# A new engine order, searched over sampled transfer delays, and Silu's table loaded by the first activation

## The chip, the cores and the metric

The kernel runs on one core of a Trainium2 chip. The metric is the device time of one execution in microseconds (us), as the median of several runs. A run is called fast or slow by how it stands to the fastest run of the same kernel, and only fast runs are compared.

## The reference

One sequence of 2048 rows with 640 columns in bfloat16 goes through two blocks, each with a residual:

```python
def _A_ref(q, k, v, shift_k, ssm_k, ssm_D):
    k_shift = ...                       # causal 4-tap filter of k along the sequence, per column
    kv = k_shift * v
    kv_f = rfft2(pad(kv));  kf_f = rfft2(pad(ssm_k))
    y = irfft2(kv_f * kf_f)[:S]         # long convolution along the sequence, per column
    return q * (y + kv * ssm_D)

def _B_ref(x, w_gate, w_up, w_down):    # 640 -> 1728 -> 640
    return (silu(x @ w_gate) * (x @ w_up)) @ w_down

h  = A_q + _A_ref(layernorm(A_q), A_k, A_v, A_shift_k, A_ssm_k, A_ssm_D)
h2 = h + _B_ref(layernorm(h), B_w_gate, B_w_up, B_w_down)
```

## The kernel before

The sequence is cut into four blocks of 512 rows. For each block the kernel forms the key-value product (`kv`), takes it through the long convolution as matmuls with transform tables, multiplies by the normalised query, normalises again and runs the feed-forward network (FFN). Between two matmul stages of the convolution the intermediate is written back to on-chip memory in another layout by small DMA transfers. I call these **reshuffles**; SyncE issues them. The convolution's filter goes through the same kind of transfer (the **filter shuffles**). A step of ACT or DVE that copies a matmul's result out of its accumulation memory is called an **evacuation**. A_k, A_v and A_q are the loads of a block's inputs.

Nothing is issued while the Python code walks through the computation. Each step is recorded with its engine, a cost, and what it reads and writes. Then a list scheduler places the steps by rank. A table of 1616 ranks and a string that fixes which of ScalarE (ACT) or VectorE (DVE) does a step were found by a search and are written into the source:

```python
_ORDER = """
156 113 119 17 19 112 121 158 111 118 482 590 193 ...     # [cut: 1616 ranks]
"""
_WHO = ("....d..ad.da.dd......................................."  # [cut]
)
...
for r, i in enumerate(_ORDER.split()):
    P.ops[int(i)].prio = r
for o, w in zip(P.ops, _WHO):
    o.force = {"a": "act", "d": "dve"}.get(w)
P.schedule(0.8)
```

The costs (in us) and the transfer's assumed times stand where a step is recorded. Nearly all steps go through such helpers, which is why the profile shows L681 for most matmuls, L672 for most transfers and L891 for most vector work:

```python
def dma(subs, kb, reads, writes, prio, eng="sp", ..., kind="load", w=None):
    return P.op({eng: (0.9 if eng == "pool" else 0.62 if kind == "shuffle" else 0.5) * len(subs)}, fns, reads, writes, prio,
                dma=((w or kb / 390.0), ..., 0.8 if kind != "load" else 1.5), name=name)

# reciprocal square root of a LayerNorm: GpSimd (POOL), between two small DVE steps va and nm
P.op({"pool": 1.05}, lambda g: g.tensor_tensor(out=y, in0=va, in1=..., op=ALU.pow), ..., name=f"nr{l}{j}")
```

The third part that matters is the key-value product of blocks 2 and 3. Three of its four taps are added by DMA, not by an engine: GpSimd issues a transfer of 320 KB that adds while it writes. The DVE step `kvv`, which multiplies by v, needs the last of these:

```python
def acc(src, cells):
    P.op({"pool": 1.0}, [lambda g: g.dma_start(v4(t0), src(), accum_op=ALU.add)],
         [(t0, 0)] + cells, [(t0, 0)], prio, dma=(2.1, 2.1, 0.8), name=f"kvd{j}{c}")
...
acc(lambda: v4(t1), [(t1, 0)])
mul(t1, 2)
... # tap 3, on DVE
acc(lambda: kw(0), [(kt, c)])
acc(lambda: v4(t1), [(t1, 0)])                     # the third: kvv waits for it
vec(dve2(W4), tt(hv, hv, lambda: v4(t0), ALU.mult), [(t0, 0), (vt, c)] + ..., name=f"kvv{j}{c}")
```

The FFN's gate goes through ACT's Silu (`si`), and DVE multiplies by the other half (`gm`).

Of the kernel before, what the change touches and what calls it, by code (L numbers as in the profile page):

```python
# [16 lines left out]
156 113 119 17 19 112 121 158 111 118 482 590 193 1380 1412 1519 464 211 432 1142 466 1146 485 1418 1408 1322 1321 53 22 1108 1134 24 28 1143 1350 87  # L17
1509 25 205 1 1377 1243 955 1430 1346 73 1347 642 153 21 30 27 29 134 798 43 63 71 167 110 115 106 9 536 57 654 956 794 1250 217 75 82 93 100 84 952
65 12 1247 376 26 3 56 97 379 378 129 102 162 760 1111 91 20 2 1121 23 15 1162 1318 1300 1354 1410 1426 130 61 31 269 406 373 37 128 96 381 450 410
588 596 492 59 6 416 501 1118 69 1330 1434 1308 528 516 518 1338 802 801 1130 163 98 86 127 546 1233 1416 542 165 1448 538 499 664 704 1031 151 67 90  # L20
941 942 225 1251 685 784 1045 550 933 1086 1096 714 228 540 548 1175 1406 1319 264 274 1444 527 169 1456 621 370 1481 1013 1381 183 728 719 669 1424
135 147 139 231 452 455 531 903 346 690 226 229 1087 985 792 999 680 1011 694 431 437 208 81 245 817 243 791 192 544 772 300 319 294 256 186 724 783
184 182 827 835 1266 1258 585 979 665 1254 1256 1264 1260 695 1009 1007 709 675 392 511 238 467 261 1114 408 420 557 32 689 699 1028 407 367 239 230
202 670 920 917 201 421 213 204 198 191 45 4 1104 790 257 244 189 598 399 423 987 415 576 137 356 782 787 786 679 1001 418 255 251 227 977 529 459
1228 1348 1109 1344 461 1116 159 232 108 469 1362 1316 1312 224 446 442 178 99 149 206 168 514 200 1043 700 387 397 55 223 524 458 426 209 267 468 428
160 141 417 517 197 526 263 520 143 171 199 190 1113 414 443 219 582 1168 157 120 1349 1172 203 1443 1357 1441 447 483 710 411 0 448 796 64 60 477 377
409 1465 1438 1351 506 389 393 487 246 1314 412 368 1141 58 1457 1352 595 809 480 500 1409 1244 1242 581 398 438 177 390 535 534 222 216 215 1274 270
1227 131 150 686 495 1119 764 556 375 207 558 241 240 247 254 1371 1364 1363 1171 564 566 577 575 1372 170 266 36 486 35 70 85 1570 154 34 1212 386
1569 276 286 1433 161 1403 117 385 775 502 145 403 507 498 572 441 1374 493 565 681 424 242 1058 470 1565 522 103 503 975 401 770 530 221 1442 1436
181 391 454 369 769 766 301 944 295 938 419 220 439 395 701 939 947 394 396 388 465 237 142 473 471 497 1563 1150 253 296 641 474 935 891 860 605 608  # L30
607 579 402 814 196 549 551 249 472 974 1440 1496 435 1040 1413 800 479 478 78 52 1089 1091 768 1353 218 433 543 1117 508 851 1432 1313 1492 1178 236
1139 1446 767 578 574 803 496 822 781 726 1063 1067 1065 973 644 328 315 1262 306 553 563 950 316 951 88 427 614 1471 1369 1345 1342 777 532 1360 1472
1466 321 314 547 613 1240 820 823 661 552 1166 1458 647 829 1439 337 855 863 1216 862 155 1485 525 212 696 1238 1464 1462 1428 1239 1358 1236 1234 505
567 374 521 523 1488 284 265 706 281 1411 1205 656 449 586 776 404 1615 774 1514 587 811 806 876 360 1588 1177 333 364 1167 425 258 456 1420 773 490
325 457 1473 195 146 233 148 948 599 476 512 324 275 268 1069 18 271 857 1487 845 11 491 949 444 771 210 895 214 1419 250 326 1523 1597 1486 1606 1453
405 365 555 1066 721 413 33 640 252 899 72 39 248 422 906 136 133 1309 1068 1084 475 1226 172 653 639 1094 1310 570 632 865 617 627 904 825 912 889 68
94 913 1106 1107 1102 1098 429 1608 305 991 989 901 897 1248 635 957 62 5 1187 101 515 881 1421 911 545 74 797 638 460 430 1375 235 589 481 969 623
930 929 1399 436 650 1246 651 1224 821 628 1217 778 965 853 309 988 440 462 83 1218 1221 655 868 636 38 92 76 591 282 914 910 907 887 1245 1378 66
1241 637 434 400 1463 1020 1235 1366 1367 1138 1468 937 1290 878 338 1037 932 509 180 351 877 793 893 659 886 981 41 819 504 843 779 445 1014 976 185
510 176 166 114 174 1497 831 756 953 609 666 867 1215 842 291 780 610 606 997 494 1291 1270 995 996 1220 1230 1140 924 1607 513 350 573 1269 1271 1272  # L40
859 14 849 164 844 1469 280 1027 871 892 347 962 1057 1041 940 705 902 890 928 1030 453 1095 1049 8 272 259 262 716 896 888 1407 353 7 1315 841 1252
915 982 619 1547 1535 1555 1263 1268 691 795 711 1257 1024 676 980 990 992 123 1103 671 925 1016 1082 126 1105 1093 788 1017 1376 1083 1081 1078 1578
1567 879 451 1577 1341 47 1382 840 1267 1015 916 1451 984 1079 173 89 175 122 1259 1261 1101 657 116 40 152 620 80 921 909 884 882 559 484 946 344
1025 519 959 625 900 894 1035 931 354 1021 1005 1018 1019 852 846 1059 1023 838 1002 986 1566 936 934 463 1155 905 604 815 290 1524 304 1072 1388 1214
1196 1255 1265 1551 1559 684 785 1527 285 1543 1158 1126 674 918 187 1539 1449 1197 805 561 124 971 1292 1219 50 873 874 77 125 537 799 1475 48 16 260
13 1003 1511 1460 1201 1522 1452 1286 1225 789 10 51 109 132 1000 569 629 1513 1454 1185 667 662 46 49 1115 1311 1004 138 1298 194 140 1253 1574 1323
1289 1326 1122 188 660 1611 54 601 1154 1211 594 600 663 107 1199 1223 278 1573 541 1561 1553 1558 1470 382 539 279 371 273 380 105 95 597 42 584 603
593 299 1537 612 615 104 1202 384 383 289 922 1229 1538 1557 1188 1181 1123 44 1609 1542 1222 1437 1429 1132 1033 1549 571 813 1459 372 1144 1541 1525
919 978 1306 1294 1355 1288 179 144 1404 1332 1074 1127 725 1398 1053 804 908 807 288 1401 1032 826 1076 1180 1505 1343 618 488 1427 630 1384 751 1278
355 489 993 983 1602 1279 1560 1572 1540 737 1529 1546 1110 366 234 1526 1213 1055 927 926 1237 1530 1550 1533 1302 1071 1075 1276 812 1287 1285 1385  # L50
568 1589 1151 1159 1135 624 970 960 964 1545 1249 866 643 583 1435 533 562 818 668 1593 1534 1562 580 1170 1390 1280 1386 1414 1008 677 1478 1373 1198
968 1128 998 1392 277 850 1394 1284 283 808 592 1333 1006 687 1450 611 954 898 1152 358 864 312 626 634 707 298 560 602 287 311 1186 1507 682 810 1010
297 1584 1595 854 292 828 1422 1336 832 967 293 302 883 830 816 652 313 885 317 836 303 824 834 308 858 1317 943 861 692 330 733 673 1012 1528 307
1585 318 327 966 331 738 1402 1077 340 322 323 958 972 1174 622 357 648 335 1482 1581 848 363 361 339 1328 1592 1383 1397 342 672 1050 678 872 336
1594 875 348 341 1461 945 1232 1048 1026 683 658 717 722 1598 1590 688 1415 1603 693 362 334 646 343 856 697 359 1320 1455 713 1554 332 1029 712 1173
1423 698 1044 702 703 1042 727 649 645 1387 1277 1393 1467 1164 1120 1080 1064 708 349 345 1334 755 746 1389 554 1340 352 1275 1056 1604 718 1613 1612
723 1092 961 1304 1052 748 765 1061 740 750 1165 1039 1169 1296 739 1359 735 1281 837 310 1176 1293 1301 1283 1273 1400 747 1370 1361 1060 741 754 994
1073 1160 1099 1508 749 1070 1054 833 633 631 1512 1521 1136 1516 1517 869 729 1062 1022 870 1034 1124 1580 1137 1447 1161 1391 1324 1046 1556 1153
1145 880 1356 1231 1112 1038 1299 1297 1335 734 715 1088 1305 1327 1325 1295 1395 1303 1036 1575 1379 736 1183 1192 1282 1051 732 731 1100 1148 1097
1480 1133 1484 1208 1194 1206 1491 1489 1090 1368 1190 753 1189 1193 1156 1531 1396 744 743 1179 752 329 1586 1582 1571 1600 1591 730 923 759 1047  # L60
1498 1479 1515 1125 1510 1085 1207 1329 1331 1579 1307 1157 1337 1149 1417 1425 742 720 1500 763 745 847 1599 1203 1339 757 758 1131 1445 839 320 616
1200 963 1474 1147 1204 1209 1191 1477 1520 1476 1163 1483 1182 1499 1493 1502 1494 1501 1490 1184 1195 1518 1504 1506 1129 1495 1503 79 1431 1405
1210 1564 762 761 1605 1601 1583 1610 1536 1532 1548 1552 1568 1614 1596 1587 1576 1365 1544
"""
_WHO = (
# [456 lines left out]
def bass_sequential_preLN__ssm_conv_h3__swiglu_ffn__prompt_kernel(  # L522
# [28 lines left out]
    P = Prog()  # L551
# [812 lines left out]
```

## Time and profile before

| | before |
|---|---|
| median, us (3 runs) | 313.04 (311.83 to 314.07) |
| span of the profiled run, us | 310.9 |
| TensorE (PE) busy, us | 284.1 (91%) |
| DVE busy, us | 243.3 (78%) |
| ACT busy, us | 194.2 (62%) |
| GpSimd (POOL) busy, us | 29.5 |
| mean granted PE clock (1 is full speed) | 0.989 |

PE is the busiest engine, but not the bound all the time. Up to about 60 us DVE is full and PE waits for it; from 210 us on PE alone is full; in between the engines hand work to each other, and a stretch of the timeline has to be read for the wait that ends last in it. The prediction below shows the stretches, the waits of the worst one and the chain that explains them. One pair of lines it does not show becomes important later. It is from the waits over the whole span (who waited for whom: us in total, times, longest us):

```profile
PE ps L681 <- DMA sb<-sb: 8.8, 9, 2.9
DVE sb L891 <- DMA sb<-sb: 4.1, 3, 2.1
```

PE loses 8.8 us to transfers within the on-chip memory, and DVE loses 4.1 us.

### The profile page before, as it was taken

The page shows a single profiled execution, that of the slowest core. Times are in us where ns is not written, and L with a number is a line of the kernel's source. Part 1 is how long each engine was busy: PE and PEld are TensorE (multiplying, and loading weights), DVE is VectorE, ACT ScalarE, POOL GpSimd, SP SyncE. Part 2 cuts the span into 40 slices and gives each one's busy share as a digit, 9 for nine tenths or more (in the row PEclk, how much of TensorE's full clock was granted, in tenths as well). Part 3 has the DMA queues.
Part 4 walks back from the last instruction along what each step waited for, and adds up shares of the span by engine and source line. Part 5 has one row for each costly group of instructions (what it writes and reads, how often), then busy time and mean ns, then how long its engine had stood idle before and what let it go on. Part 6 is the DMA issues. An engine that isn't in the chain of part 4 may idle for free.

```text
span 310.9 us, 5160 instructions
## 1 busy us (share of the span) xinstructions
PE 284.1 (91%) x1804; PEld 152.7 (49%) x1804; DVE 243.3 (78%) x493; ACT 194.2 (62%) x450; POOL 29.5 (9%) x34
## 2 busy tenths in 40 slices
PE   3799887989989989999499999989999999999995
PEld 1466554434534456653234465534444576444563
DVE  5899999988799969998759999996599672313421
ACT  3389999998877626986668985695983220332100
POOL 2101102031101204200101020200010010000000
PEclk9999999899999999999979999999999999999999
DMA  7999996748907795558500261674201105000002
GB/s 209 362 373 273 364 358 216 235 113 203 234 3 211 147 289 115 129 159 228 142 1 2 84 126 44 233 132 146 86 0 42 44 20 128 23 0 0 2 14 71
DMA packets 42473, 43.24 MB, mean 139 GB/s; under 512 B 14848, under 2 KB 37056, under 8 KB 42320
## 3 DMA queue, kind: packets, MB, share of 16 engines
q1 hardware_dynamic: 38974, 38.30, 40.2%
q0 software_dynamic: 3328, 3.97, 8.0%
q10 hardware_dynamic: 146, 0.66, 0.6%
q8 instruction: 14, 0.23, 0.3%
q14 instruction: 11, 0.09, 0.1%
HBM read 20.63 MB, written 2.62 MB: 75 GB/s over the span
## 4 chain that ended last, share of the span: by engine, by line
PE 55%; DVE 18%; DMA 15%; ACT 5%; SPq 3%; issue 2%; POOL 0%; DVEq 0%; ACTq 0%; POOLq 0%
PE ps L681 54%; DVE sb L891 15%; DMA sb<-sb 13%; SPq L672 3%; ACT sb L664 3%; DMA sb<-in_A_ssm_k_dram 2%; ACT sb L1027 1%; DVE stt L981 1%; DVE sb L665 1%; PE ps L798 1%; PE ps L1199 1%; DVE sb L1153 1%; POOL stt L997 0%; ACT L1223 0%; ACT sb L1223 0%
## 5 line engine op out<-in xcount | busy, mean ns | idle before, releaser
L681 PE MATMUL ps<-sb 128*128 128x320 bf16 (+2 forms) x1204 | 224.7, 340 | 8.6 <-POOL stt L970 2.8
L891 DVE TENSOR_TENSOR sb<-sb 128x1280 bf16<-128x1280 bf16 (+3 forms) x270 | 166.0, 672 | 8.5 <-DMA sb<-sb 4.1
L681 PEld LDWEIGHTS ps<-sb 128*128 128x128 bf16 (+2 forms) x1204 | 115.0, 99 | 101.8 <-issue 8.4
L664 ACT ACTIVATE sb<-ps 128x320 bf16<-128x320 f32 (+2 forms) x246 | 100.4, 489 | 38.9 <-PE ps L681 32.9
L681 PE MATMUL ps<-sb,tab 128*64 128x320 bf16 (+2 forms) x512 | 66.4, 309 | 12.2 <-DMA sb<-sb 7.7
L891 DVE TENSOR_TENSOR sb<-ps,sb 128x320 bf16<-128x320 f32 (+2 forms) x70 | 38.6, 572 | 43.3 <-PE ps L681 31.1
L1223 ACT ACTIVATE sb<-ps 128x512 bf16<-128x512 f32 (+1 forms) x56 | 33.5, 602 | 37.2 <-PE ps L681 37.1
L681 PEld LDWEIGHTS ps<-sb,tab 128*64 128x64 f16 (+2 forms) x512 | 32.0, 102 | 46.7 <-issue 15.2
L1007 ACT ACTIVATE sb<-sb,stt 128x320 bf16<-128x320 bf16 (+1 forms) x40 | 28.2, 739 | 11.2 <-DVE stt L999 11.1
L997 POOL TENSOR_TENSOR stt<-stt 128x2 f32<-128x2 f32 (+1 forms) x12 | 13.5, 1124 | 120.7 <-DVE stt L996 66.7
L665 DVE CAST sb<-ps 128x320 bf16<-128x320 f32 x41 | 19.0, 482 | 5.7 <-PE ps L681 5.5
L1067 POOL DMA_DIRECT2D sb<-sb x12 | 12.2, 1016 | 78.1 <-DVE sb L891 57.4
L667 ACT ACTIVATE sb<-ps 128x320 bf16<-128x320 f32 x42 | 16.3, 459 | 4.4 <-PE ps L681 4.1
L981 DVE BATCH_NORM_STATS2 stt<-sb 128x6 f32<-128x320 bf16 x32 | 14.2, 476 | 0.0
L1027 ACT ACTIVATE sb<-sb,stt 128x640 bf16<-128x640 bf16 x16 | 13.4, 835 | 0.5 <-DVE stt L1023 0.5
L1020 ACT ACTIVATE sb<-sb 128x640 bf16<-128x640 bf16 x16 | 11.9, 746 | 1.4 <-DMA sb<-in_A_q_dram 1.4
L798 PE MATMUL ps<-sb 128*128 128x128 bf16 (+1 forms) x48 | 4.0, 231 | 2.2 <-DMA sb<-in_A_ssm_k_dram 2.1
L798 PEld LDWEIGHTS ps<-sb 128*128 128x128 bf16 (+1 forms) x48 | 3.2, 120 | 3.7 <-DMA sb<-in_A_ssm_k_dram 2.7
L1199 PE MATMUL ps<-sb 128*128 128x128 bf16 x40 | 4.1, 242 | 0.6 <-DVE sb L1006 0.6
L809 POOL TENSOR_TENSOR sb<-sb 1x320 bf16<-1x320 bf16 x2 | 2.2, 1108 | 24.1 <-ACT sb L664 17.5
L1199 PEld LDWEIGHTS ps<-sb 128*128 128x128 bf16 x40 | 2.8, 106 | 2.5 <-DVE sb L1006 0.8
L668 DVE TENSOR_SCALAR sb<-ps 128x320 bf16<-128x320 f32 x6 | 2.9, 489 | 0.9 <-PE ps L681 0.9
(23 smaller groups left out, 29.3 us busy)
## 6 DMA issues: line engine op xcount, KB each, us to landing
sb<-sb SPq DMA_DIRECT2D x72, 160.0 KB, 2.2
sb<-sb POOLq DMA_DIRECT2D x12, 320.0 KB, 4.3
out_dram<-sb SPq DMA_DIRECT2D x16, 160.0 KB, 2.0
sb<-in_A_k_dram SPq DMA_DIRECT2D x8, 280.0 KB, 4.2
sb<-in_B_w_down_dram SPq DMA_DIRECT2D x13, 160.0 KB, 7.2
sb<-cst_den SPq DMA_DIRECT2D x8, 256.0 KB, 7.8
sb<-in_A_q_dram SPq DMA_DIRECT2D x6, 320.0 KB, 4.5
sb<-in_A_v_dram SPq DMA_DIRECT2D x6, 320.0 KB, 5.5
```

Of the source, the lines that this page charges most:

```text
L664: fns = {"act": lambda a: a.activation(out=dst(), in_=src(), func=ACTF.Copy), "dve": lambda v: v.tensor_copy(out=dst(), in_=src())}
L665: "dve": lambda v: v.tensor_copy(out=dst(), in_=src())}
L667: fns = {"act": lambda a: a.activation(out=dst(), in_=src(), func=ACTF.Copy, scale=scale), "dve": lambda v: v.tensor_scalar(out=dst(), in0 ...
L681: return lambda t: t.matmul(o(), l(), r(), start=st, stop=sp)
L891: return lambda v: v.tensor_tensor(out=o(), in0=a(), in1=b_(), op=op)
L981: vec(dve1(CW, False), lambda v: v.bn_stats(st6(l, j, b, c), V(xt, b * D + c * CW, CW)), [(xt, (b, c))], [(ST, ("s", l, j, b, c))], prio, ...
L997: P.op({"pool": 1.05}, lambda g: g.tensor_tensor(out=y, in0=va, in1=stt[:, 420:420 + hi - lo], op=ALU.pow), c1 + [(ST, "half")], c3, prio, ...
L1007: "act": lambda a: a.activation(out=dst(), in_=src(), func=ACTF.Identity, scale=rs(l, j, b), bias=tmv(l, j, 3)[:, b:b + 1])},
L1020: P.op({"act": act_c(D) + 0.22}, lambda a, b=b, jt=jt: a.activation(out=V(jt, 0, D), in_=V(xt, b * D, D), func=ACTF.Copy, accum_out=tmv(l, ...
L1027: P.op({"act": act_c(D) + 0.3}, lambda a, b=b, jt=jt: a.activation(out=V(jt, 0, D), in_=V(xt, b * D, D), func=ACTF.Square, bias=tmv(l, j, ...
L1067: P.op({"pool": 1.0}, [lambda g: g.dma_start(v4(t0), src(), accum_op=ALU.add)], [(t0, 0)] + cells, [(t0, 0)], prio, dma=(2.1, 2.1, 0.8), n ...
L1223: P.op({"act": act_c(n)}, lambda a: a.activation(out=dst(), in_=src(), func=ACTF.Silu), rd, wr, -1000, name=f"si{nm}", after=after)
```

## The change

The intent: the search that makes the order no longer minimises the span for one nominal set of transfer times. It minimises the mean span over samples of them, so that an order that is fast only if each transfer takes its nominal time is marked down. Three costs that the scheduler assumes are raised, and a tiny Silu is put ahead of everything, so that ACT loads Silu's table while nothing waits for it.

```diff
 _ORDER = """
-156 113 119 17 19 112 121 158 111 118 482 590 193 ...    [cut: all 1616 ranks]
+59 1571 1566 12 3 1574 93 71 61 1575 1570 73 57 ...      [cut: all 1617 ranks]
 _WHO = (
-    "....d..ad.da.dd....."   [cut]
+    ".....a.a..ad.aa....."   [cut: seven steps change from DVE to ACT, net]
@@ def dma
-  ... 0.8 if kind != "load" else 1.5), name=name)
+  ... 0.8 if kind != "load" else 2.0 if name[0] in "xv" or name[:3] == "kin" else 1.5), name=name)
@@ def ln_rstd
-            P.op({"pool": 1.05}, lambda g: g.tensor_tensor(... op=ALU.pow), ...
+            P.op({"pool": 1.2}, lambda g: g.tensor_tensor(... op=ALU.pow), ...
@@ def acc
-                P.op({"pool": 1.0}, [lambda g: g.dma_start(v4(t0), src(), accum_op=ALU.add)],
+                P.op({"pool": 1.35}, [lambda g: g.dma_start(v4(t0), src(), accum_op=ALU.add)],
@@ def load_weights
+            P.op({"act": 0.3}, lambda a: a.activation(out=V(WD, 13 * D, 8, 64, 128), in_=V(WD, 13 * D, 8, 64, 128), func=ACTF.Silu),
+                 [(WD, (13, "z"))], [(WD, (13, "z"))], -3000, name="sil0")
```

## The prediction

> **What bounds the kernel now.** The list of busy times on the profile's page comes first: TensorE (PE) is busy 284.1 of 310.9 us, so at most 26.8 us of the span has an idle PE, and no new order can take more than that plus what PE loses while it counts as busy. The second view cuts the span into stretches and shows when it is idle; its columns are the stretch, its length, then the busy time and (instructions) of PE, weight loads, DVE, ACT, POOL, then clock, DMA share and GB/s.
>
> ```profile
> 0.00:10.00 10.00, 3.80 (x20) 1.88 (x20) 5.72 (x12) 3.30 (x5) 2.35 (x9) 1.00 0.81 236
> 10.00:60.00 50.00, 45.04 (x315) 27.39 (x316) 49.37 (x110) 42.42 (x105) 5.37 (x5) 0.97 1.00 320
> 60.00:130.00 70.00, 65.26 (x428) 33.75 (x428) 62.85 (x127) 52.73 (x122) 12.37 (x11) 1.00 0.63 155
> ...
> 140.00:160.00 20.00, 14.57 (x76) 5.71 (x74) 14.02 (x25) 11.88 (x30) 0.84 (x1) 0.91 0.52 144
> 160.00:190.00 30.00, 29.96 (x189) 15.61 (x189) 29.81 (x57) 26.80 (x65) 3.40 (x3) 1.00 0.24 55
> 190.00:210.00 20.00, 17.84 (x139) 10.12 (x136) 19.51 (x46) 14.31 (x35) 1.92 (x2) 1.00 0.60 160
> 210.00:300.00 90.00, 89.92 (x527) 46.95 (x528) 49.10 (x102) 33.55 (x69) 2.37 (x3) 1.00 0.14 42
> 300.00:311.00 11.00, 7.70 (x57) 5.31 (x55) 2.95 (x6) 0.00 (x0) 0.00 (x0) 1.00 0.17 60
> ```
>
> Length less PE busy gives the idle ledger: 6.2 us at the start, 5.0 in 10-60, 4.7 in 60-130, 5.4 in the twenty microseconds 140-160, 2.2 in 190-210, 3.3 at the end, and nothing in the rest. Start and end (first loads; last evacuation and store) are hardly open to an order. In 10-60 DVE is busy 49.4 of 50 us and ACT 42.4, so there PE waits for vector work. From 210 to 300 PE alone is the bound. The stretch to read closely is 140-160. The waits of that stretch (who waited for whom: total us, times, longest):
>
> ```profile
> PE ps L681 <- DMA sb<-sb: 5.4, 2, 2.9
> ...
> DVE sb L891 <- DMA sb<-in_A_v_dram: 2.7, 1, 2.7
> ACT sb L1020 <- DMA sb<-in_A_q_dram: 1.4, 1, 1.4
> ```
>
> All its PE idleness is two waits for on-chip reshuffles (the transposes of the convolution's intermediate between its stages). The chain of waits says why they were late:
>
> ```profile
> 144.13 0.55 SPq L672
> ...
> 144.78 5.27 DMA sb<-sb
> ...
> 150.13 0.56 SPq L672
> 150.74 0.60 SPq L672
> 151.38 0.61 SPq L672
> ...
> 152.03 4.12 DMA sb<-sb
> ```
>
> A reshuffle has a median of 2.2 us from issue to landing in the table of issues; these took 5.27 and 4.12. The timeline shows SyncE issuing A_q loads at 139.71 and A_v loads at 143.06, just ahead of them in the same queue. There is a second loss that PE's busy share hides: the clock column reads 0.91 there. 46 matmuls of 512 columns took 12.0 us in 140-160 (261 ns each), against 48 in 10.5 us in 270-280 (219 ns): 46 x 0.042 = 1.9 us. So the stretch loses 5.4 + 1.9 = 7.3 us.
>
> The table load of Silu is one row, taken from the source view of that line:
>
> ```profile
> L1223 ACT ACT_TABLE_LOAD  x1: 1283/1283/1283, 61.6 to 61.6; - x1
> ```
>
> It stands in the chain that ended last, at 61.58, in a stretch (60-70) where ACT was busy 9.97 of 10 us; soon after it PE waits for ACT 0.67 and 0.37 us (66.12 and 66.94).
>
> **What the Trainium skill says.** "ScalarE: Activation LUTs", section "What ACT_TABLE_LOAD costs", gives about 1283 ns for the load plus about 1380 ns of drain for every switch of set. The trace agrees on the load (1283 ns, twice) and shows no drain: the previous ACT item ended at 61.57, the load began at 61.58, and the first Silu followed at 62.88. I use 1.28 us. "DMA: Bandwidth & Descriptors", in the latency part on where the ~2 us go, puts a small transfer at about 2 us fixed; the 2.2 us median agrees. The same page, "Queues, rings and completion order", says that on each DMA engine descriptors are consumed in ring order; the 5.27 us of a reshuffle issued behind four large loads agrees. "TensorE: Matmul & The Clock Gate", Part 1, says that an idle window of about 3.4 us halves the PE clock until a busy window follows; the 0.91 behind gaps of 2.9 and 2.5 us fits, though neither gap is a whole window.
>
> **The change part by part.** The work is the same: 500 PE steps in both orders, 493 DVE steps become 486 and 418 ACT steps 426 (eight evacuations change hands, one Silu on eight columns is new). The three altered cost constants only feed the scheduler. What moves is order, and I read it by counting the matmuls that stand between two points on PE, at 0.219 us per 512 columns and 320/512 of that (0.137) for 320.
>
> 1. *The loads ahead of block 2's last reshuffles.* The A_v buffer comes free when the last stage-1 matmul of block 2 has read it. Before, from there to the second pair of inverse transforms stand two groups of five 512-column matmuls and one pair: 2.5 us. In the new order stand nine 320-column, twenty 512-column and ten 320-column matmuls: 1.2 + 4.4 + 1.4 = 7.0 us. Besides, the four 80 KB shuffles of the next filter, which stood mixed among the loads on SyncE at 0.6 us an issue, now follow the reshuffles: 2.4 us of issue out of the way. So the loads should be down before the reshuffles are issued. The reshuffle itself still has only 4.4 us of PE work to hide behind (4.9 before), and its own path is an evacuation (0.5), issues (0.6 each, two) and 2.2 landing, near 4 us. I keep 2.8 of the 7.3 us as lost. **Gain 4.5 us**; the DVE wait of 2.7 us for A_v should go with it.
> 2. *Silu's table.* The tiny first activation waits only for a memset that ends at 2.7 us before, and the first real ACT work starts at 3.56, so the load is free at the start. 1.28 us leave ACT at 61.6. PE shows 1.04 us of waits on ACT behind it. **Gain 0.8 us.**
> 3. *190-210.* PE waits 1.17 us for the transposed normalised rows at 210.01 and 0.5 us for ACT at 193.74. Between the last inverse transform and the first FFN group that needs those rows there are 14.2 us of PE work now, 11.1 before. **Gain 1.0 us.**
> 4. *The early phase, bound by DVE.* DVE work up to the second transposed evacuation of block 0, by the mean durations of the rows, falls by about 0.9 us. The reshuffle of block 1's first half now has 7.9 us of PE work to hide behind, 2.3 before, where two waits of 0.28 and 0.16 us stood. **Gain 0.9 us.**
> 5. *What gets worse.* SyncE now issues a small w_down load before the very first filter load: one issue, **0.5 us lost**, since the filter's landing at 7.25 us starts the chain. Two reshuffles in 60-110 have less cover (7.7 to 5.1 us and 6.8 to 4.1 us), and one inverse reshuffle 5.3 to 4.5 us where PE already waited 1.07: **0.8 us lost.**
>
> Sum: 4.5 + 0.8 + 1.0 + 0.9 - 0.5 - 0.8 = 5.9 us. From the median of 313.04 that is 307.1. A search over sampled delays has presumably also closed small gaps that I did not count; I take 0.3 us for them: **306.8 us**.
>
> **The rivals.** *A new wait takes the old one's place.* PE only reaches later work sooner; if the reshuffles are late for their own path (4.4 us of cover against some 4 us) rather than for the loads ahead, most of the 7.3 us stays. For it: the cover shrank by half a microsecond. Against: 5.27 us for a transfer whose median is 2.2 says queueing. It would leave 311 us. *DVE keeps the pace.* In 160-190 DVE is busy 29.8 of 30 us and PE 29.96; work gained at 150 may be handed back by DVE at 200, where it is busy 19.5 of 20. For it: DVE's total of steps up to block 3's products falls by only some 3 us. It would give 309 to 310. *The search did better than my ledger.* It had 17 us of idle time in the middle plus clock losses to work on, and averaging over delays penalises just the tight spots; were half of it gone, 303 us. *The transfers were hidden anyway* is ruled out for 140-160, since PE itself shows the wait, but holds for the last 78 us, where nothing can be won.
>
> **Range and chances.** The range runs from the third rival (some 301.5) to the first with a little loss elsewhere (312.0). The 2% line is at 306.8, my own number, so faster by over 2% and within 2% are near even: 0.48 and 0.49. A slowdown of over 2% would need a new serial wait of 6 us; 0.03.
>
> **What would show it.** One table load only, in the first 4 us, and none near the first Silu of the FFN (part 2). Around 130-160 PE idle of at most 3 us, no DVE wait for A_v, the reshuffles landing in under 3 us, the clock at 0.95 or more (part 1). PE idle under 1.2 us in 190-210 (part 3). The first filter landing some 0.5 us later (part 5). PE idle in all near 21 us. I would be wrong if the idle of 140-160 turns up again as DVE or DMA waits at 200, if the tighter reshuffles in 60-110 cost over 2 us, or if the extra load at the start pushes the whole DVE-bound phase back by more than one issue.

## The result, and the profile after

| | before | after |
|---|---|---|
| median, us (4 runs each) | 312.44 (309.94 to 314.07) | 303.20 (301.88 to 304.50) |
| span of the profiled run, us | 310.9 | 301.2 |
| PE busy, us | 284.1 (91%) | 278.9 (93%) |
| DVE busy, us | 243.3 | 240.6 |
| ACT busy, us | 194.2 | 194.2 |
| GpSimd busy, us | 29.5 | 33.5 |
| mean granted PE clock | 0.989 | 0.994 |

The ratio is 0.9711 with a 95% interval of 0.9631 to 0.9791. All outputs are right. A ratio here is the mean time of one kernel's fast runs over the mean of the other's fast runs of the same rounds, so it is not quite the ratio of the medians. The trace after has 18 of the 1804 matmul records missing (the weight loads are complete), so its PE busy time is read a little low.

The stretches of the kernel after, with the columns that the prediction explains (stretch, length, busy time and instructions of PE, weight loads, DVE, ACT and POOL, then clock, DMA share, GB/s):

```profile
0.00:10.00 10.00, 3.95 (x20) 1.75 (x20) 4.16 (x8) 4.61 (x10) 2.52 (x9) 1.00 0.78 241
10.00:60.00 50.00, 42.14 (x304) 26.68 (x305) 48.64 (x113) 42.22 (x104) 8.96 (x7) 0.97 0.96 322
60.00:130.00 70.00, 67.47 (x448) 35.67 (x452) 66.11 (x130) 53.67 (x129) 9.84 (x9) 1.00 0.66 160
...
140.00:160.00 20.00, 18.73 (x96) 8.22 (x98) 19.07 (x36) 17.94 (x43) 5.65 (x4) 1.00 0.47 109
160.00:190.00 30.00, 29.51 (x204) 15.92 (x207) 30.00 (x63) 24.16 (x63) 0.72 (x1) 1.00 0.28 93
190.00:210.00 20.00, 19.89 (x144) 10.79 (x145) 15.15 (x30) 15.17 (x35) 1.27 (x1) 1.00 0.49 138
210.00:290.00 80.00, 78.84 (x456) 41.70 (x460) 44.24 (x93) 27.74 (x57) 3.72 (x3) 1.00 0.11 33
290.00:301.20 11.20, 8.42 (x62) 5.84 (x60) 3.21 (x7) 0.00 (x0) 0.00 (x0) 1.00 0.17 59
```

Length less PE busy is PE's idle time. In 140-160 it fell from 5.4 to 1.3 us, and the clock there rose from 0.91 to 1.00. In 190-210 it fell from 2.2 to 0.1 us. In 10-60 it rose, from 5.0 to 7.9 us. Note DVE too: in 140-160 it was busy 14.0 us and is now busy 19.1 us; in 190-210 it was full with 19.5 us and now has 4.9 us to spare.

The waits over the whole span, after:

```profile
PE ps L681 <- DMA sb<-sb: 2.2, 2, 1.5
```

PE's wait for on-chip transfers fell from 8.8 to 2.2 us. DVE's line of 4.1 us for such transfers is gone, and so is its wait of 2.7 us for A_v.

The source view of the new activation:

```profile
L1220 ACT ACT_TABLE_LOAD  x1: 1283/1283/1283, 1.7 to 1.7; - x1
L1220 ACT ACTIVATE sb<-sb x1: 205/205/205, 3.0 to 3.0; 64x8 bf16<-64x8 bf16 x1
```

There is one table load, at 1.7 us, and none at the first Silu.

**Where the time came from.** Stretches of equal time hold different work in the two orders, so idle times by the clock do not tell where one order draws ahead. I therefore counted weight loads of PE, each weighted by the columns of its matmul (0.219 us per 512 columns, the prediction's figure), and noted when each order has reached the same amount of PE work:

| PE work done, us | reached before, us | order after is ahead by, us |
|---|---|---|
| 35 | 56 | -2.9 |
| 55 | 80 | +0.1 |
| 105 | 139 | +1.9 |
| 115 | 152 | +4.3 |
| 125 | 167 | +8.0 |
| 145 | 188 | +5.9 |
| 155 | 200 | +7.6 |
| 165 | 214 | +10.5 |
| end | 311 | about +9.5 |

The new order is **behind** by 2.9 us at 56 us, back to level at 80, gains 6.1 us between 139 and 167, loses 2.1 us, and gains another 4.6 us up to 214. The gains and losses by stage add up to the 9.5. A recount of the same loads, with the matmuls on the transform tables at 0.65 of their columns, moves single points by up to 0.8 us (the end to 9.2) and leaves the pattern as it is. Differences between runs at equal work below that name this recount are taken from it.

A milestone on DVE's side is the second power of block 2's LayerNorm, since it needs all DVE work of block 2 before it. From the timelines of GpSimd (start, duration, instruction, idle time before it and what ended that), before:

```profile
200.94 1.20 POOL L997 TENSOR_TENSOR stt<-stt 128x2 f32<-128x2 f32 x1 [1.55 <-DVE stt L996]
```

and after:

```profile
190.44 1.27 POOL L997 TENSOR_TENSOR stt<-stt 128x2 f32<-128x2 f32 x1 [1.60 <-DVE stt L1036]
```

It comes 10.5 us earlier. Up to it DVE was busy 182.3 us before and 178.4 us after, and idle 18.6 and 12.0 us. So 6.6 of the 10.5 us are idle time of **DVE** that went away, although DVE is not the engine with the highest busy share.

### The profile page after: what moved, and what is told of

The parts are those of the page before. It is cut to its first block, busy times and chain, and to the rows that moved or that the text cites. A ratio compares the mean times of both kernels' runs of the same rounds, so it can differ in the third digit from the quotient of the medians.

```text
span 301.2 us, 5136 instructions
## 1 busy us (share of the span) xinstructions
PE 278.9 (93%) x1786; PEld 151.7 (50%) x1804; DVE 240.6 (80%) x486; ACT 194.2 (64%) x457; POOL 33.5 (11%) x34
## 4 chain that ended last, share of the span: by engine, by line
PE 50%; DVE 35%; DMA 5%; issue 3%; POOL 3%; ACT 2%; SPq 1%; DVEq 0%; ACTq 0%
PE ps L681 49%; DVE sb L891 30%; DMA sb<-sb 3%; POOL stt L997 3%; DVE stt L981 2%; DMA sb<-in_A_ssm_k_dram 2%; DVE sb L665 2%; DVE sb L1153 1%; ACT sb L664 1%; ACT sb L667 1%; PE ps L1199 1%; ACT sb L1007 1%; SPq L672 1%; PE ps L798 0%; DVE sb L1006 0%
## 5 line engine op out<-in xcount | busy, mean ns | idle before, releaser
L681 PE MATMUL ps<-sb 128*128 128x320 bf16 (+2 forms) x1186 | 222.4, 338 | 10.9 <-POOL sb L697 2.3
L891 DVE TENSOR_TENSOR sb<-sb 128x1280 bf16<-128x1280 bf16 (+3 forms) x270 | 165.6, 672 | 1.2 <-ACT sb L667 0.8
L681 PEld LDWEIGHTS ps<-sb 128*128 128x128 bf16 (+2 forms) x1204 | 114.3, 99 | 102.1 <-DVE sb L891 5.3
L664 ACT ACTIVATE sb<-ps 128x320 bf16<-128x320 f32 (+2 forms) x257 | 104.2, 481 | 29.0 <-PE ps L681 22.1
L891 DVE TENSOR_TENSOR sb<-ps,sb 128x320 bf16<-128x320 f32 (+2 forms) x70 | 38.9, 573 | 43.1 <-PE ps L681 28.1
L681 PE MATMUL ps<-sb,tab 128*128 128x320 bf16 (+2 forms) x512 | 66.5, 306 | 4.5 <-DMA sb<-sb 2.2
L681 PEld LDWEIGHTS ps<-sb,tab 128*128 128x128 f16 (+2 forms) x512 | 32.0, 101 | 37.4 <-issue 14.1
L1007 ACT ACTIVATE sb<-sb,stt 128x320 bf16<-128x320 bf16 (+1 forms) x36 | 25.1, 731 | 14.8 <-DVE stt L999 13.4
L997 POOL TENSOR_TENSOR stt<-stt 128x2 f32<-128x2 f32 (+1 forms) x12 | 16.1, 1346 | 116.0 <-DVE stt L996 80.3
L665 DVE CAST sb<-ps 128x320 bf16<-128x320 f32 x29 | 13.4, 482 | 5.8 <-PE ps L681 5.8
L809 POOL TENSOR_TENSOR sb<-sb 1x320 bf16<-1x320 bf16 x2 | 3.6, 1796 | 21.1 <-ACT sb L664 14.6
L1006 DVE TENSOR_SCALAR sb<-sb,stt 128x320 bf16<-128x320 bf16 (+1 forms) x12 | 4.6, 400 | 0.1
L999 DVE TENSOR_TENSOR stt<-stt 128x2 f32<-128x2 f32 (+1 forms) x12 | 1.8, 149 | 3.1 <-POOL stt L997 3.1
(23 smaller groups left out, 29.5 us busy)
```

Source lines behind the costliest of these rows:

```text
L664: fns = {"act": lambda a: a.activation(out=dst(), in_=src(), func=ACTF.Copy), "dve": lambda v: v.tensor_copy(out=dst(), in_=src())}
L665: "dve": lambda v: v.tensor_copy(out=dst(), in_=src())}
L681: return lambda t: t.matmul(o(), l(), r(), start=st, stop=sp)
L891: return lambda v: v.tensor_tensor(out=o(), in0=a(), in1=b_(), op=op)
L997: P.op({"pool": 1.2}, lambda g: g.tensor_tensor(out=y, in0=va, in1=stt[:, 420:420 + hi - lo], op=ALU.pow), c1 + [(ST, "half")], c3, prio, ...
L1007: "act": lambda a: a.activation(out=dst(), in_=src(), func=ACTF.Identity, scale=rs(l, j, b), bias=tmv(l, j, 3)[:, b:b + 1])},
```

## The experiments

An edit of the ranks alone moves much else, because the scheduler then chooses buffers anew. So for the experiments I wrote the order out as one list of step numbers for each engine, and each engine takes the next step of its list:

```diff
-  for o in sorted((o for o in ready if e in o.engs and o.force in (None, e) and ...), key=lambda o: (o.prio, o.idx)):
+  for o in (o for o in ready if o.force == e and o.prio == len(order[e]) and ...):      # rank = place in this engine's list
```

Written so, both kernels give the same instructions, buffers and semaphore counts as the originals. Lines of the source stand two higher in most of these kernels (L683 is L681, L893 is L891). Each experiment was timed in five rounds against the kernel before, whose fast runs had a median of 311.7 to 312.1 us in these rounds; each own median is of six runs. Each profile is one execution. Against the line of 2%, e7 and e8 are faster than the kernel before, e1, e3, e4 and e5 count as the same, and the others are unclear; the intervals given are of 95%.

The three raised costs cannot be tried together without the new order: before's ranks with after's costs, and the reverse, run out of buffers in the scheduler and never complete. In the finished program a cost is nothing but the order it leads to, so all tests are of the order.

Theory at the start: the time comes from block 2's loads and reshuffles (part 1 of the prediction), some from 190-210. Rivals: the new early phase does it; or the late order does it; or DVE's lateness does it.

### Four hybrids: which stretch of the new order is worth what

**e1_old_start**: before's order until 58 us, after's from there; no first Silu.

```diff
 pe, act, dve, pool, sp lists:
+  [steps that before's schedule starts before 58 us, in before's order]
+  [all other steps, in after's order]
```

> Engine orders of before up to the first FFN groups (some 58 us), of after from there. Read at equal TensorE work, after is 1.6 us behind before at 60 us and 9 to 10 us ahead at the end. Theory that the stages are independent: the old start removes the 1.6 us lag, so 301.6 us, 1.6 below after. Rival, that the lag is an investment (DVE does block 1's key-value product first, and gets it back in 60-120): 304 us or more, slower than after.

Measured: 307.10 us (305.98 to 307.90), ratio 0.9858 (0.9802 to 0.9915). This is 3.9 us *slower* than after, although the new early phase is 2.9 us behind at 56 us. The seam shows in PE's timeline:

```profile
67.33 1.68 PE L683 MATMUL ps<-sb 128*128 128x512 bf16 x5 [4.12 <-ACT sb L1225]
```

PE waits 4.12 us for ACT at one point. Part of the loss may thus come from my seam, so I mended it:

**e11_old_start_mended**: e1 with the first Silu, and with the first two Silus of the FFN ahead of block 1's LayerNorm on ACT.

```diff
 act list:
   0 18
+  261          # the first, tiny Silu
   11 7 ...
+  si01, si010  # moved ahead of block 1's LayerNorm sums
```

> Old start until 58 us, new order after, with the seam mended: the table of Silu loaded first, and two FFN Silus ahead of the block-1 normalisation on ACT, so that the 4.1 us wait of TensorE for ACT seen at the seam goes. If the seam alone cost the time: 307.1 - 4 = 303 us, or 302 with the table load off the path, at or below after. If the new start is an investment (2.6 us of DVE work done ahead): 304.5 us or more.

Measured: 305.81 us (305.26 to 306.68), ratio 0.9802 (0.9758 to 0.9846). Mending won 1.3 us, of which the table load can be 0.7 (e7 below). Yet PE still waits, now 3.54 us for DVE at 68.24 us, and DVE waits 3.46 us for ACT just before. By the recount at equal work, e1 and e11 both fall some 5 us behind the kernel before between 56 and 70 us, at the seam: the mend moved the wait and did not remove it. So the two runs do not tell the worth of the new early phase from the cost of the seam. That this phase is an investment (it does some 2.6 us more of block 1's key-value work on DVE before block 0's LayerNorm, PE is late for that, and the order that follows needs it done) fits the table above, but it is argued and not shown.

**e2_old_until_124** and **e3_new_until_124**: the orders exchanged at 124 us, one each way.

```diff
 e2: + [steps before 124 us in before's order]  + [the rest in after's order]
 e3: + [steps before 124 us in after's order]   + [the rest in before's order]
```

> Order of before up to about 124 us, of after from there. Stages independent: the gains of 140-160 (5.8), 160-185 (-2.0), 185-210 (+4.7) and the tail (-0.5) remain, 8.0 in all: 304.4 us. Rival, that the late gains need the lead built up before 124: 308 us or more.

> Order of after up to about 124 us, of before from there. Stages independent: only the 1.6 us lead at 124 remains, 310.8 us, with the two reshuffle waits of the old 140-160 (5.4 us of idle TensorE) back in the trace. Rival, that the old order only waited because it came late to that stage: under 307 us.

Measured: e2 306.35 us (305.26 to 308.03), ratio 0.9839 (0.9779 to 0.9898); e3 310.78 us (310.11 to 311.42), ratio 0.9982 (0.9927 to 1.0037). The order from 124 us on is worth 5.5 us by itself (311.90, the median of the fast runs of before, to 306.35), and the first 124 us only 1.1 us (311.90 to 310.78), which the interval does not tell from nothing. The waits of 136-162 in e3 show that the old loss is back:

```profile
PE ps L683 <- DMA sb<-sb: 4.5, 2, 2.5
```

**e4_old_until_180**: before's order until 180 us, after's from there.

```diff
+  [steps before 180 us in before's order]  + [the rest in after's order]
```

> Order of before up to about 180 us, of after from there. By the equal-work reading the stage 185-210 is worth 4.7 us and the tail -0.5: 308.2 us. By the prediction's part 3 it is worth 1.0 us: 311.4 us.

Measured: 314.86 us (312.68 to 317.17), ratio 1.0111 (1.0027 to 1.0195). Both expectations missed: the late order alone gains nothing and costs about 1%. Its stretch 190-210 and its milestone:

```profile
190.00:210.00 20.00, 16.52 (x122) 9.35 (x120) 17.17 (x41) 11.46 (x27) 1.99 (x2) 0.92 0.50 149
```

```profile
200.60 1.27 POOL L999 TENSOR_TENSOR stt<-stt 128x2 f32<-128x2 f32 x1 [2.63 <-DVE stt L1038]
```

With the loads and reshuffles of the old order, block 2's LayerNorm is as late as before (200.60 against 200.94), and PE then idles even more, 3.5 us. So the late order gains nothing at 190-210 while DVE is late (a cost of the seam at 180 us may be in this). Whether DVE's earlier time alone is enough is answered by e12 below: it is not.

Hence 140-160 was the place to take apart.

### Two ways to get the reshuffles of block 2 on time

**e5_old_loads_early**: the kernel before, with part 1 of the prediction done in full. The last stage-1 matmul group of block 2 and its evacuation move up (the A_v buffer comes free earlier), A_v and A_q are issued first, and four filter shuffles go behind the reshuffles.

```diff
 pe list:  354 986
+978 
           667 662 ... 1253 663
-978
 act list: 355 993
+979
           669 664 ... 1254 665
-979
 sp list:  347 356
-1228 -1227                  # filter shuffles
+1220 +1219                  # loads
           783 782
-1230 -1229 -1220 -1219
           923 922 ... 996 994
+1228 +1227 +1230 +1229
```

**e9_old_shuffles_behind**: the kernel before, with only those four shuffles moved behind the reshuffles on SyncE. No buffer comes free earlier and no load is issued out of its order.

```diff
 sp list:  347 356
-1228 -1227
           783 782
-1230 -1229
           1220 1219 923 922 ... 996 994
+1228 +1227 +1230 +1229
```

> Before, with one place changed: the last stage-1 group of block 2 (and its evacuation) moved up from behind two FFN groups, so that the A_v buffer comes free some 5 us earlier; A_v, then A_q loads issued at once; the four filter shuffles behind the last reshuffles. Theory that the loads ahead of the reshuffles are the cause: the two waits of 5.4 us and the DVE wait of 2.7 us for A_v go, and with DVE no longer late part of the 4.6 us at 190-210 as well: 306 us (304 to 308). Rival, that the reshuffles' own path sets the time or that DVE gives it back: 311 us or more.

> Before with SyncE's order alone changed: the four filter shuffles, whose wait for TensorE held the A_q and A_v loads back in the queue, go behind the last reshuffles; nothing moves on TensorE, so the A_v buffer comes free as late as before. If the shuffles at the head of the queue are the cause: as good as the run with both changes, 3 us below before, 309 us. If the late buffer is the cause: 312 us, A_v still lands at 149 and the reshuffles behind it.

Measured: e5 308.85 us (307.86 to 310.71), ratio 0.9905 (0.9860 to 0.9951); e9 308.35 us (304.92 to 309.33), ratio 0.9852 (0.9793 to 0.9911). PE's wait for reshuffles in 136-162, 5.4 us in the kernel before, is 0.5 us in e5 and gone in e9. The time of e5 lies between its two expectations. In e5 the work from 105 to 125 is 6.5 us faster, about what the kernel after gains there. And e9 does as well with the shuffles alone. SyncE's lines in e9 (the issue of A_v, then that of the reshuffles):

```profile
143.17 1.95 SPq L674 DMA_DIRECT2D sb<-in_A_v_dram  x2
...
146.54 3.89 SPq L674 DMA_DIRECT2D sb<-sb  x3
```

A_v now goes out 3.4 us ahead of the reshuffles, against 1.1 us in the kernel before (143.06 and 144.13), and the first two reshuffles land a median of 2.4 us after their issue, against 5.4 us. So the loads stood in the reshuffles' way, as part 1 said; and of its two halves **the four shuffles ahead in SyncE's queue were what held the loads back**, while the earlier-freed buffer adds nothing that can be seen.

But 6.5 us gained in the stretch became only 3.1 us in the time of e5 and 3.8 us in that of e9 (medians of fast runs). The timeline of e9 shows where the rest went (GpSimd's issue of the third accumulating transfer, the DVE step that needs it, the matmuls that need that):

```profile
106.75 0.86 POOL L1069 DMA_DIRECT2D sb<-sb  x1 [4.56 <-DMA sb<-sb]
...
114.83 0.82 DVE L893 TENSOR_TENSOR sb<-sb 128x1280 bf16<-128x1280 bf16 x1 [5.47 <-DMA sb<-sb]
...
116.31 3.92 PE L683 MATMUL ps<-sb 128*128 128x320 bf16 x14 [4.17 <-DVE sb L893]
```

e5, the same DVE step:

```profile
114.81 0.82 DVE L893 TENSOR_TENSOR sb<-sb 128x1280 bf16<-128x1280 bf16 x1 [4.57 <-DMA sb<-sb]
```

and the kernel before:

```profile
107.17 0.86 POOL L1067 DMA_DIRECT2D sb<-sb  x1 [4.29 <-DMA sb<-sb]
...
112.68 0.83 DVE L891 TENSOR_TENSOR sb<-sb 128x1280 bf16<-128x1280 bf16 x1 [1.71 <-DMA sb<-sb]
```

From issue to use it is 5.5 us in the kernel before, 7.6 in e5, 8.1 in e9; in e2 and e4 it was 5.7 and 6.1. All five have the same order up to this point. So **one transfer takes between 5.5 and 8.1 us with the same program ahead of it**, and DVE stands still for it, 1.7 us in the best of these profiles and 5.5 us in the worst. What made it long in e5 and e9 is not known. The kernel after has this:

```profile
105.61 0.86 POOL L1067 DMA_DIRECT2D sb<-sb  x1 [3.89 <-DMA sb<-sb]
...
114.34 0.77 DVE L891 TENSOR_TENSOR sb<-sb 128x1280 bf16<-128x1280 bf16 x1
```

There the step is placed 8.7 us behind the issue, with other DVE work in between, and DVE does not wait at all (the transfer landed 6.1 us after its issue). This was a theory that I had not had when I predicted, and it can be tried with one step:

**e12_old_two_mends**: e9, and on DVE the step `kvv21` (number 957, the last key-value product of block 2) some 5 us later in the list.

```diff
 dve list: 625 959
-957
           329 326 ... 636 639
+957
           1245 641
```

> Before with the four filter shuffles behind the reshuffles (as in the run before, 308.35 us) and one DVE instruction moved: the last key-value product of block 2, which reads what GpSimd's accumulating transfer brings, goes from 3.8 us to some 9 us behind that transfer's issue, about where the new order has it. In five profiles of the old order the transfer took 5.5, 5.7, 6.1, 7.6 and 8.1 us from issue to use, and DVE stood 1.7 to 5.5 us. Theory that this exposure to transfer delay is what the new search removed: the DVE wait there under 0.5 us in the profile, 306 us, and runs closer together. Rival, that DVE's idle time there costs nothing because TensorE has work: 308 us, the same as without it.

Measured: 304.69 us (303.88 to 305.34), ratio 0.9757 (0.9712 to 0.9802). This is better than I had expected. DVE's wait for the transfer is gone from the waits of 100-122. Its stretches:

```profile
140.00:160.00 20.00, 19.61 (x106) 8.84 (x107) 20.00 (x38) 18.23 (x44) 2.04 (x2) 1.00 0.39 110
...
190.00:210.00 20.00, 18.19 (x131) 9.44 (x130) 16.59 (x35) 15.97 (x38) 1.92 (x2) 1.00 0.52 155
```

and its milestone:

```profile
192.36 1.20 POOL L999 TENSOR_TENSOR stt<-stt 128x2 f32<-128x2 f32 x1 [1.55 <-DVE stt L998]
```

PE idles 0.4 us in 140-160 (5.4 before), block 2's LayerNorm comes 8.6 us earlier than before, and DVE has 3.4 us of 190-210 to spare. Five moved steps thus bring the old order within 1.5 us of the new one: four shuffles are worth 3.8 us by the medians of fast runs (312.12 to 308.35) and 4.6 us by the ratio, and one DVE step is worth 3.7 us more on top of them (308.35 to 304.69; 3.1 us by the means; in different calls, whose fast runs of the kernel before had medians of 312.12 and 311.71). The step was not tried without the shuffles.

The same profile shows what the old order still lacks. DVE is now nearly as early as in the kernel after, but the stretch 190-210 has the old order, and PE waits there for the transposed normalised rows as it did before. The kernel before, then e12:

```profile
210.01 2.32 PE L681 MATMUL ps<-sb 128*128 128x512 bf16 x10 [1.17 <-DMA sb<-sb]
```

```profile
201.74 3.18 PE L683 MATMUL ps<-sb 128*128 128x512 bf16 x14 [1.49 <-DMA sb<-sb]
```

In the kernel after and in e2, which have the new order there, PE has no such wait. By the recount, after and e2 both gain 3.9 us between 188 and 214 us, and e12 gains 0.4. So the gain at 190-210 takes both: DVE on time (e4) and the new order of that stretch (e12).

The spread of the times speaks the same way. The standard deviation of the six runs is 1.77 us in e9 and 0.55 us in e12. It is 1.5 us over the 27 fast runs of the kernel before in these experiments. The runs of e9 fall into two groups, 304.9 and 305.9 against 308.3 to 309.3, and its profile is of the slower one. But e5, which has the same DVE step as early, has only 1.04 us. Six runs are few, so this is weak support and no proof.

### Undoing parts of the new order

**e6_new_loads_late**: the kernel after, with its last stage-1 group of block 2 (the group that frees A_v's buffer) two FFN groups later, and A_q ahead of A_v.

**e10_new_loads_at_reshuffle**: the same group moved to just ahead of the inverse transforms, so that A_v is issued at 140.0 us and the reshuffles at 141.7 us.

```diff
 e6, pe list:   661 989
-991
                336 337 ... 1256 1268
+991
                663 673
 e10, pe list:  663 673
+991
                1258 920
 both, act list: step 992 (its evacuation) likewise; sp list: A_q (783, 784) ahead of A_v (1220, 1221)
```

> After, with the reverse: its last stage-1 group of block 2 put behind the two first FFN groups, A_q issued ahead of A_v; the filter shuffles stay behind. Theory of the loads: waits for reshuffles or A_v come back around 140-150 and the time goes up by 3 us or more, 306 us and above. Rival, that the rest of the new order carries the gain: under 304.2 us.

> After with its last stage-1 group of block 2 moved further back, to just ahead of the second pair of inverse transforms, A_v last of the four loads, so that A_v is issued right ahead of the reshuffles as in before (1 us, against 3 us in the run with the milder move, which cost 1 us). Theory of the loads: reshuffle waits of 3 to 5 us and a DVE wait for A_v come back at 140-150, 307 us or more. Rival, that the new order has slack there whatever the loads do: under 305 us.

Measured: e6 304.59 us (302.20 to 305.41), ratio 0.9756 (0.9710 to 0.9802), 1.4 us slower than after, between its two expectations and with no reshuffle wait; the loads were still 3 us ahead. e10 307.01 us (304.52 to 307.73), ratio 0.9828 (0.9781 to 0.9875), so 3.8 us slower than after. The time hits the expectation of the theory that the loads must be out of the way, but the profile does not show it done in the way that was expected. The waits of 136-162 in e10:

```profile
DVE sb L893 <- DMA sb<-in_A_v_dram: 1.7, 1, 1.7
...
PE ps L683 <- DMA sb<-sb: 0.3, 1, 0.3
```

DVE's wait for A_v is back, but PE waits for reshuffles only 0.3 us there, not 3 to 5. At equal work e10 is already 4.0 us behind the kernel before at 35 us of PE work, against 2.9 for after, where the order has not been edited. So part of the loss in that profile lies in a place that the edit does not touch. By the recount e10 is 2.5 us behind after by 139 us, and loses another 1.8 us between 139 and 167, about DVE's wait for A_v. I count e10 as inconclusive for the whole 3.8 us. What it shows is that late loads bring DVE's wait back, and not PE's: the first two reshuffles took 3.9 us to land there (3.1 in after), but PE had work meanwhile.

**e7_new_no_table_first**: the kernel after without the first Silu.

```diff
-            P.op({"act": 0.3}, lambda a: a.activation(out=V(WD, 13 * D, 8, 64, 128), in_=..., func=ACTF.Silu), ..., name="sil0")
```

> After without the tiny first activation, all engine orders the same: the first copy loads a table without Silu and Silu's 1.28 us load stands again before the first FFN Silu. By the prediction 0.8 us slower, 304.0 us. Rival 1, that ACT is on the path and all 1.28 us count: 304.5. Rival 2, that it is hidden there: 303.2.

Measured: 303.89 us (303.16 to 304.77), ratio 0.9743 (0.9701 to 0.9784). That is 0.7 us over after by the medians, which fits the predicted 0.8, though runs of one kernel scatter by as much. The load is back in front of the first Silu:

```profile
L1225 ACT ACT_TABLE_LOAD  x1: 1283/1283/1283, 62.7 to 62.7; - x1
```

**e8_new_dve_waits_pow**: in the kernel after, the power of a LayerNorm on GpSimd took up to 2.9 us, where before it took at most 1.6. A guess was that DVE's work on other things holds GpSimd up, so the edit puts DVE's next LayerNorm step (`nm`) directly behind `va` for blocks 2 and 3, and DVE has to wait for the power.

```diff
 dve list:
   va02
+  nm02
   ...
-  nm02
   va03
+  nm03
   ...
-  nm03
```

> After, with DVE held idle during two of GpSimd's powers (128x4) of blocks 2 and 3, by moving the DVE instruction that uses the power directly behind the one that feeds it. In after these took 2.61 and 2.32 us, in before 1.20 and 1.01. Theory that DVE's running instructions slow the power down: both take about 1.0 us, the waits of 1.16 us (158.75) and 0.85 us (227.88) on TensorE shrink, 302 us. Rival, that the length has another cause (what GpSimd did before): they stay over 2 us and DVE idles over 2 us each time, 304 us or more.

Measured: 303.39 us (302.70 to 305.30), ratio 0.9731 (0.9683 to 0.9778), no gain. The power of block 2's or 3's rows in after, the same in e8, and in e7, whose DVE order is after's:

```profile
154.17 2.61 POOL L997 TENSOR_TENSOR stt<-stt 128x4 f32<-128x4 f32 x1 [0.53 <-DVE stt L996]
```

```profile
154.91 1.03 POOL L999 TENSOR_TENSOR stt<-stt 128x4 f32<-128x4 f32 x1 [0.53 <-DVE stt L998]
```

```profile
154.97 1.03 POOL L999 TENSOR_TENSOR stt<-stt 128x4 f32<-128x4 f32 x1 [0.53 <-DVE stt L998]
```

The short power came as expected in e8, but it came in e7 as well, without the edit. So the guess is not supported, the cause of the long ones stays open, and it costs no time that could be seen.

| kernel | median, us | ratio to before | what it told apart |
|---|---|---|---|
| after | 303.20 | 0.971 | |
| e8 | 303.39 | 0.973 | long powers cost nothing |
| e7 | 303.89 | 0.974 | table load: 0.7 us |
| e6 | 304.59 | 0.976 | loads 3 us ahead: no reshuffle wait |
| e12 | 304.69 | 0.976 | five moved steps: nearly all |
| e11 | 305.81 | 0.980 | old start, mended |
| e2 | 306.35 | 0.984 | order from 124 us on: 5.5 us |
| e10 | 307.01 | 0.983 | late loads: some 1.8 us |
| e1 | 307.10 | 0.986 | old start, with a seam |
| e9 | 308.35 | 0.985 | four shuffles: 3.8 us |
| e5 | 308.85 | 0.991 | buffer and loads add nothing |
| e3 | 310.78 | 0.998 | first 124 us: within noise |
| before, fast runs | 311.7 to 312.1 | 1 | |
| e4 | 314.86 | 1.011 | late order alone: no gain |

No version beats the kernel after.

## Why the prediction was right or wrong

The range held the result, and the direction was right; the chances had put "within 2%" a hair higher than "faster", and it came out faster. The point lay 3.6 us too high, and the parts behind it fared differently. That the sum came no further off was partly luck, since parts 4 and 5 were both wrong, with opposite signs. A count in the prediction is off too: not eight but seven steps change hands, net (493 to 486 on DVE); nothing rests on it.

- **Part 1, the loads ahead of block 2's reshuffles: mechanism right in one half, size too small.** Predicted 4.5 us, with 2.8 of 7.3 us kept as lost; at equal work the stretch gained 6.1 us. The step that failed is the kept loss: I held the reshuffle's own path of near 4 us against 4.4 us of cover and expected to see some of it, but PE's wait there nearly vanished (no wait for a reshuffle in 136-162 of after). The clock went to 1.00 (predicted 0.95 or more), the A_v wait of DVE went; the first two reshuffles landed in 3.1 us, not under 3. Of the two causes I named, e9 shows that taking the 2.4 us of shuffles out of SyncE's queue was enough; the earlier-freed buffer, to which I gave the longer working, showed no gain of its own (e5 against e9).
- **Part 2, Silu's table: right.** 0.8 us predicted, 0.7 by e7, within the scatter.
- **Part 3, 190-210: cause right as far as it went, a condition missed, the term too small.** I expected 1.0 us from more PE work between the inverse transform and the first FFN group. At equal work the order gained 4.6 us in 188-214, after giving 2.1 us back just before, so 2.5 us net. The wait of 1.17 us that I named is gone in after, and stays in e12 (1.49 us), which has the old order there. What I missed is that this order pays only when DVE is on time: in e4 it gains nothing. DVE reaches block 2's LayerNorm 10.5 us earlier in after, and PE has work at once.
- **Part 4, the early phase: wrong in sign.** A gain of 0.9 us was predicted; the order is 2.9 us behind at 56 us. I compared two places and two waits, not what else had been moved in: some 2.6 us of block 1's work on DVE. That the following part needs it fits e1 and e11, whose seam keeps it from being shown.
- **Part 5, what gets worse: wrong.** The first matmuls on the filter started at 7.08 us (7.29 before), although the filter's issue moved from 0.74 to 1.40 us, so one issue more in front of a load made no delay that can be seen (over the other profiles this start varies from 6.5 to 8.2 us with the old start and from 7.1 to 7.7 us with the new). The reshuffles with less cover in 60-110 cost nothing visible either: PE's idle time in 60-130 fell from 4.7 to 2.5 us, and at equal work this stage gained.
- **What the sum did not contain.** DVE's wait for the accumulating transfer, 1.7 us in the profile of before and up to 5.5 us in others of the same order, which e12 shows to be worth 3.7 us when it is taken out on top of the shuffles. The line stood in the waits of the kernel before. I had left it out because I kept a ledger of PE's idle time only: in that profile PE did not wait for DVE there, while in e9 it lost 4.2 us at once. The summed parts gave 6.2 us (with the 0.3 for small gaps); up to 139 us the order gained 1.9 in place of 0.4 (parts 2, 4 and 5), in 139-167 it gained 6.1 in place of 4.5, in 167-214 2.5 in place of 1.0, and it lost 1.0 after that, which is the 9.5.
- **The rivals.** A new wait did not take the old one's place. *DVE keeps the pace* came out reversed: DVE is the engine through which the gain was kept, since it stood still for transfers and stopped doing so. *The search did better than my ledger* is the one that came nearest, at 303 us, and I gave it too little weight: an order made for the mean over delays should work against just those waits of which one profile shows only one sample (argued, not shown).

What stays open: how much each raised cost did (not tried); what makes up the last 1.5 us between e12 and after (the wait of 1.49 us that e12 keeps is a candidate, and was not tried); what e10 loses before 139 us; why the accumulating transfer takes 5.5 us at one time and 8.1 at another; and why GpSimd's power takes 1.0 us at one time and 2.6 at another. That the samples in the search, rather than the raised cost of the accumulate's issue, led to the later place of `kvv21` is argued from the stated intent and not shown.

## What to carry to other kernels

Ask of each transfer how far its use stands behind its issue, and hold that against the longest time that several profiles show, not against the median: the transfer that held DVE for 1.7 us in one profile here held it for 5.5 us in another of the same order. Look in the queue of the engine that issues transfers for things that nobody needs yet standing in front of what the bound engine needs next. And keep a ledger of idle time for every engine that feeds the bound one, because its lost time can come back as the bound engine's wait elsewhere: here the new order of 190-210 paid only once DVE had lost 6.6 us less before it.

## What the Trainium skill lacked or had wrong

- "DMA: Bandwidth & Descriptors", section "Anatomy of one DMA — SWDGE (gpsimd) path", fits the time of a transfer that GpSimd issues as 2.0 us plus its bytes over 436 GB/s. For 320 KB that would be an estimate of 2.8 us. The accumulating transfers here have a median of 4.3 us from issue to landing, and one of them took 5.5 to 8.1 us from issue to use in five profiles with the same order before it. The page gives no spread, and the spread is what this change was about.
- The same page, "Queues, rings and completion order", gives the ring order on the DMA engines, but not what that costs at the issuing queue: four 80 KB shuffles in front of the reshuffles made the kernel 3.8 us slower by the medians (e9 against before).
- "ScalarE: Activation LUTs", section "What ACT_TABLE_LOAD costs": the stated drain of some 1380 ns was not to be seen beside the 1283 ns of the load; taking the load off the path gained 0.7 us (e7 against after).
- "TensorE: Matmul & The Clock Gate", Part 1, speaks of an idle window of about 3.4 us. Gaps of 2.9 and 2.5 us, neither a full window, already stood beside a mean granted clock of 0.91 in 140-160; with gaps that add up to 1.3 us it was 1.00. A gap of 4.2 us agrees with the page: the clock was 0.81 in 104-122 of e9.
- No page that I looked up gives a time for GpSimd's power on a 128x4 tile; the same instruction took 1.0 or 2.6 us here.
